# Gate and value products of the first MoE by Strassen's seven block products, with joins kept in PSUM and one ring of weight buffers

## The chip, the cores and the metric

The kernel runs on one core of a Trainium2 chip. The engines of the core are PE (TensorE: matmuls), DVE (VectorE), ACT (ScalarE), POOL (GpSimd) and SP (SyncE, which issues the loads and stores); each works through its own instructions in order. Matmul results are written to PSUM, in banks of 2 KB a partition; everything else lies in SBUF. The metric is the time of one execution on the device in microseconds, as a median over several runs.

## The reference

An attention over clusters (2 batches, 8 heads, 768 positions) gives 1536 tokens of 512 features. Two MoE layers follow, both in fp32:

```python
def _moe_ref(x, w_gate, w_val, w_out, rms_g):       # 512 -> 1536 -> 512
    rms = np.sqrt(np.mean(x * x, axis=-1, keepdims=True) + 1e-06)
    xn = x / rms * rms_g
    g = xn @ w_gate
    silu = g * (1.0 / (1.0 + np.exp(-g)))
    val = xn @ w_val
    return (silu * val @ w_out).astype(np.float32)

def _moe2_ref(x, w_in, w_out, s, b):                # 512 -> 2048 -> 512
    h = x @ w_in
    r = np.maximum(h, 0.0)
    g = s * (r * r) + b
    return (g @ w_out).astype(np.float32)
```

The weights come as 64-bit floats; the kernel turns them to 32 bits itself.

## The kernel before, in words

**Products.** An fp32 product is made of three fp32r matmuls: each operand is split in a high part (ACT copies it to fp32r) and a low part (operand less high part, on POOL or DVE), and high x high, high x low and low x high are summed in PSUM. The tokens form four blocks `t` of 384 (`TB`), the d_ff features tiles `f` of 128, and two neighbouring tiles are a pair `fs`. A gate and value unit (`unit1`, matmuls in `mm3`, L728) of one `f` and one `t` is 24 matmuls. A projection (`proj`, `project_mm`, L740 in the first MoE, L742 in the second) of one pair and one `t` is 24 matmuls in the first and 18 in the second; DVE adds each of its results to `acc` (L750).

**Weights.** A weight tile is loaded as raw 64-bit words (`load_w`, SP), ACT makes two ramps of its top bytes (L710, L711), DVE two bit operations (L713, L716) that give the 32-bit value, then ACT makes the high and POOL the low part (L719, L722). `add_pair` does this for a pair of w_in tiles of the second MoE, with the sums of weight blocks that Strassen's method needs (L1158 to L1181).

**Strassen in the second MoE.** `quad2` computes a pair `fs` for half the tokens (two blocks `t`, together `u`) by seven block products of 6 matmuls (L1395), 42 in place of 48. It holds five banks: the first product is copied to SBUF by ACT (L1418), DVE joins the others to it (L1413), and the results are finished from there: ReLU and square (L1424, L1427, L1430), scale and shift on ACT (L1434), and the split in `gh` and `gl` (L1241, L1244) for the projection. The sums of input blocks ("forms", `forms_` and `forms_last`) are made once for each `u`.

**Order.** Up to about 288 us a planner (`Plan`, `pl`) orders the attention together with the first two pairs of the first MoE for the first two blocks `t`. What follows is ordered by `Post`, which fills each engine's queue by earliest start and due time from written-in durations; PE's order is that in which the code adds the steps. An operation given to `either` goes to POOL, or to DVE where it would end sooner by more than `GAIN` (0). The loop over `items` at the end sets PE's order: for each pair of the first MoE and each `t` two units, then the projection of the `t` before; then for each pair of the second MoE and `u` a group of `quad2`, then the projections of the `u` before. Weight buffers are two sets, one for each second item (`s`).

## Time and profile before

| | |
|---|---|
| median of 3 runs | 806.29 us (803.33 to 806.7) |
| the profiled execution | 807.27 us, its span 805.5 us, granted clock 0.994 |
| attention with the first units | 0 to about 290 us |
| first MoE | about 290 to 541 us |
| second MoE | about 541 to 803 us |

A row of the chain of waits reads: start in us, length in us, engine, tile written, line, number of instructions run together. A group row reads: line, engine, operation, what is written and read, shape, count, busy time in us and mean ns of one, then idle time in front of it and what ended that. `po` and `pg` are PSUM banks, `hv`, `th` temporary tiles, `wa`, `wb` the weights in work. A row of the windows has the count of instructions in brackets behind each busy time; PEclk is the granted clock of TensorE as a share of full speed.

### The profile page before, as it was taken

Reading aid. Unit: us, or ns where it says so; the run is one execution under the profiler, and the core shown is the slowest. Engines: PE = TensorE matmul, PEld = TensorE weight load, DVE = VectorE, ACT = ScalarE, POOL = GpSimd, SP = SyncE. Lnnn points to the kernel's source line nnn. Section 1 sums busy time; section 2 is a strip of 40 time slices with the busy share of each in tenths; the row PEclk is TensorE's granted clock in tenths of the full one; section 3 lists DMA queues with packets and bytes.
Section 4 is the critical chain, followed back from the end, with each engine's and each line's share of the span. In section 5 each row is a group of like instructions: output and inputs, shape, how many; then the busy total and the mean of one; then the engine's idle time right before and its main releaser. Section 6 shows DMA issues by size and latency. Waiting matters only on the chain.

```text
span 805.5 us, 14231 instructions
## 1 busy us (share of the span) xinstructions
PE 765.4 (95%) x5409; PEld 704.2 (87%) x5409; DVE 616.2 (76%) x979; ACT 470.4 (58%) x901; POOL 461.3 (57%) x418
## 2 busy tenths in 40 slices
PE   3899999899999899999999999998999999999998
PEld 1688876789998889999999999997888888988986
DVE  6899887988776657777755646598888878889775
ACT  5478798657757635564533413456656666576541
...
GB/s 116 93 137 119 136 172 124 64 121 118 107 108 32 49 27 121 109 111 108 128 79 27 106 27 53 53 1 26 27 53 79 74 57 77 56 79 52 53 2 156
DMA packets 98820, 65.14 MB, mean 81 GB/s; under 512 B 64992, under 2 KB 89664, under 8 KB 98752
## 3 DMA queue, kind: packets, MB, share of 16 engines
...
## 4 chain that ended last, share of the span: by engine, by line
PE 77%; DVE 10%; POOL 7%; issue 3%; ACT 2%; DMA 1%; SPq 0%; DVEq 0%; POOLq 0%; ACTq 0%
PE pg L728 23%; PE po L742 16%; PE pg L1395 11%; PE po L740 9%; PE mps L515 4%; PE pv L586 3%; PE sps L546 3%; POOL al L563 3%; PE sps L547 2%; DVE mt L523 2%; PE pv L576 2%; PE pg L740 2%; DVE wa L713 1%; POOL ah L557 1%; DVE xn L640 1%
## 5 line engine op out<-in xcount | busy, mean ns | idle before, releaser
L1244 POOL TENSOR_TENSOR gl<-hv,gh 128x384 fp32r<-128x384 f32 x73 | 82.5, 1135 | 119.5 <-ACT gh L1241 119.5
L563 POOL TENSOR_TENSOR al<-a,ah 128x768 f16<-128x768 f32 x80 | 135.6, 1712 | 18.9 <-ACT ah L559 18.1
L722 POOL TENSOR_TENSOR wl<-wa,wh 128x512 fp32r<-128x512 f32 x58 | 75.7, 1308 | 104.3 <-ACT wh L719 94.2
L728 PE MATMUL pg<-xh,wh 128*128 128x384 f32 x384 | 130.1, 339 | 2.6 <-DVE xl L656 1.4
L728 PE MATMUL pg<-xh,wl 128*128 128x384 f32 x384 | 129.2, 337 | 0.0
L728 PE MATMUL pg<-xl,wh 128*128 128x384 f32 x384 | 129.0, 336 | 0.0
L750 DVE TENSOR_TENSOR acc<-po,acc 128x512 f32<-128x512 f32 (+1 forms) x156 | 97.1, 625 | 37.7 <-PE po L742 19.3
L552 ACT ACTIVATE a<-sps 128x384 f32<-128x384 f32 x192 | 86.2, 488 | 30.7 <-PE sps L547 28.4
L523 DVE TENSOR_REDUCE mt<-mps 128x1 fp32r<-128x768 f32 x96 | 90.2, 947 | 13.8 <-PE mps L515 12.7
L728 PEld LDWEIGHTS pg<-xh,wh 128*128 128x128 f32 x384 | 72.6, 189 | 3.5 <-DVE xl L656 1.7
L742 PE MATMUL po<-wh,gl 128*128 128x512 f32 x192 | 75.0, 391 | 0.0
L742 PE MATMUL po<-wl,gh 128*128 128x512 f32 x192 | 75.0, 390 | 0.0
L742 PE MATMUL po<-wh,gh 128*128 128x512 f32 x192 | 74.7, 389 | 0.0
L546 PE MATMUL sps<-q 128*128 128x384 f32 x192 | 70.7, 368 | 3.7 <-DVE ot L497 1.7
L728 PEld LDWEIGHTS pg<-xl,wh 128*128 128x128 f32 x384 | 72.6, 189 | 0.0
L1241 ACT ACTIVATE gh<-hv 128x384 fp32r<-128x384 f32 x104 | 52.7, 519 | 34.0 <-DVE hv L1232 33.0
L728 PEld LDWEIGHTS pg<-xh,wl 128*128 128x128 f32 x384 | 72.5, 189 | 0.0
L713 DVE SCALAR_TENSOR_TENSOR wa<-wb,wa 128x512 int32<-128x512 f32 x52 | 53.2, 1023 | 18.9 <-ACT wb L711 13.3
L547 PE MATMUL sps<-q 128*128 128x384 f32 x192 | 64.7, 337 | 0.0
L515 PE MATMUL mps<-q 127*128 127x384 f32 x192 | 56.8, 387 | 5.0 <-DVE mt L523 2.9
L719 ACT ACTIVATE wh<-wa 128x512 fp32r<-128x512 f32 x58 | 36.3, 628 | 35.6 <-DVE wa L716 29.1
L586 PEld LDWEIGHTS <-ah 128*128 128x128 f16 x960 | 47.3, 98 | 7.0 <-issue 5.9
...
## 6 DMA issues: line engine op xcount, KB each, us to landing
...
```

Of the source, the lines that this page charges most:

```text
L515: nc.tensor.matmul(ps[:, e, 0:HALF], lhsT=x[0:127, 1, c * 128:c * 128 + 128], rhs=x[0:127, 2, e * HALF:(e + 1) * HALF], start=True, stop=T ...
L523: nc.vector.tensor_reduce(out=mt_of[i][:, c:c + 1], in_=m_t.pop((i, c))[:, :, 0:HALF], axis=AX.XY, op=ALU.max)
L546: nc.tensor.matmul(ps[:, 0:HALF], lhsT=x[:, 2, ks], rhs=x[:, 1, cs], start=True, stop=False)
L547: nc.tensor.matmul(ps[:, 0:HALF], lhsT=x[:, 3, ks], rhs=x[:, 0, cs], start=False, stop=True)
L552: act(out=a_t[i, c][:, e * HALF:(e + 1) * HALF], in_=s_t.pop((i, c, e))[:, 0:HALF], func=ACTF.Exp, scale=scale)
L563: nc.gpsimd.tensor_tensor(out=al, in0=a_t.pop((i, c)), in1=ah_t[i, c], op=ALU.subtract)
L728: nc.tensor.matmul(ps, lhsT=a[:, kk * 128:kk * 128 + 128], rhs=x[:, kk, :], start=(kk == m == 0), stop=(kk == KC - 1 and m == 2),)
L740: nc.tensor.matmul(ps, lhsT=a[:, cs], rhs=x, start=st[0], stop=st[1])
L742: nc.tensor.matmul(ps, lhsT=x[:, cs], rhs=a, start=st[0], stop=st[1])
L750: tt(out=ac, in0=ps, in1=ac, op=ALU.add)
L1244: two(eng)(out=gl, in0=src(), in1=gh.bitcast(F32), op=ALU.subtract)
L1395: nc.tensor.matmul(B(x), lhsT=a[:, k_ * 128:k_ * 128 + 128], rhs=b[:, k_], start=(not more and k_ == m == 0), stop=(k_ == 1 and m == 2), s ...
```

## The change

Outside the attention, the gate and value products of the first MoE are computed by Strassen's method too, one group of 42 matmuls (`quad`) for the gate and one for the value of a pair and a half `u` of the tokens: 9 of these (pair, `u`), 18 groups. Pair 1 for `t` 2 and 3 stays plain. `quad` serves both MoEs; its last three joins write to the PSUM bank that they read, and `gate1`, `val1` or `finish2` takes the result from there. `forms1` makes the input forms from the high and low parts that exist; those for `u` 0, first half, are added to the attention's planner. Weights of gate and value go through `add_pair`; all split weights share a ring of 24 tiles (`slot`). `Post` starts from the times at which the first planner ends each engine, and `GAIN` is 0.75. `finish2` has ACT make the ReLU and DVE the square, from PSUM, for all results of the second MoE. The core of the diff:

```diff
-GAIN = 0.0
+GAIN = 0.75
...
+    def forms1(u, add, lone, ks=(0, 1)):
+
+
+        def alloc():
+            views(1, u, (xh[2 * u], xl[2 * u]), (xh[2 * u + 1], xl[2 * u + 1]), new_e(u))
+            C[1, u, "t1"] = C[1, u, "12"]
+
+        e = (f"e{u}", 1)
+        if 0 in ks:
+            add("AL", 0.0, alloc, lone[0], [e, *(lone[1])], [e])
+        for k_ in ks:
+            x = lambda name, k_=k_: [at(1, u, name, y, k_) for y in "hl"]
+            xk = lambda name, k_=k_: x_keys(u, 1, name, (k_,))
+            T = Temps(add, (1, u, k_), to=lambda name, k_=k_: [z[:, k_] for z in C[1, u, name]], keys=xk, e=e)
+            T.sum("tA", *x("12"), xk("12"), ALU.add, new=True)
+            T.sum("tB", *x("11"), xk("11"), ALU.add, new=True)
+            T.sum("tA", "tA", "tB")
+            T.sum("tC", *x("22"), xk("22"), ALU.add, new=True)
+            T.sum("tC", "tC", "tA")
+            T.split("tC", "t2")
+            T.sum("tB", "tC", "tB")
+            T.split("tB", "t3")
+            T.split("tA", "t1", ([xk("12")[0], *lone[2]], [xk("12")[1], *lone[3]]))
+            T.sum("tA", *x("21"), xk("21"), ALU.add, new=True)
+            T.sum("tA", "tC", "tA")
+            T.split("tA", "t4")
...
+        def split(self, name, form, more=((), ())):
+            src, key, (hk, lk) = self.of(self.key[name]), self.key[name], self.keys(form)
+
+            def hi():
+                act(out=self.to(form)[0], in_=src(), func=ACTF.Copy)
+
+            def lo(on):
+                h, l = self.to(form)
+                two(on)(out=l, in0=src(), in1=h.bitcast(F32), op=ALU.subtract)
+
+            self.add("ACT", .52, hi, [key, self.e], [hk, *more[0]])
+            self.add("POOL", 1.08, lo, [key, hk], [lk, *more[1]])
...
+    def last_pv():
+        att_b.close()
+        expp[0] = pool(ctx, "exp0", side="right")
+        spare.append(pool(ctx, "spare", side="right"))
...
+    def slot(n=[0]):
+
+
+        n[0] += 1
+        name = f"w{'hl'[(n[0] - 1) % 2]}{(n[0] - 1) % 6 // 2}"
+        return wp[(n[0] - 1) % 24 < 12].tile([128, 512], F32R, tag=name, name=name)
...
         def room(x):
-            temp[2, n, u, x] = tp[names[x]].tile([128, TB], F32, tag="hv", name="hv")
-
-        def join(to, x, y, op=ALU.add, turn=False):
+            temp[q, x] = tp[x == "u3"].tile([128, TB], F32, tag="hv", name="hv", bufs=2 - (x == "u3"))
+
+        def join(to, x, y, sign=1.0):
+            at, k_ = (lambda: V(to), vk[to]) if to in vk else (lambda: B(to), gk[to])
             def fn():
-                if to not in (y,):
+                if to != y and to in vk:
                     room(to)
-                a, b = (V(y), B(x)) if turn else (B(x), V(y))
-                tt(out=V(to), in0=a, in1=b, op=op)
-            then("DVE", .56, fn, [gk[x], vk[y]], [vk[to]], () if to == y else [vk[to]])
+                if sc == sign == 1.0:
+                    tt(out=at(), in0=B(x), in1=V(y), op=ALU.add)
+                else:
+                    stt(out=at(), in0=B(x), scalar=sc * sign, in1=V(y), op0=ALU.mult, op1=ALU.add)
+            then("DVE", .56, fn, [gk[x], vk[y]], [k_], [k_] if to in vk and to != y else ())
 
         def copy():
             room("u2")
-            act(out=V("u2"), in_=B("a"), func=ACTF.Copy)
...
+        def fin(x, p, t):
+            finish(fs[p], t, p, lambda: B(x), gk[x], 1.0 if x != "a" else sc)
 
         t0, t1 = 2 * u, 2 * u + 1
         prod("a", "11", "11")
...
         prod("c", "s3", "t3")
         join("u3", "c", "u2")
         prod("a", "12", "21", True)
-        finish(0, lambda: B("a"), gk["a"], "c11", 0, fs[0], t0)
+        fin("a", 0, t0)
         prod("d", "s1", "t1")
-        join("c22", "d", "u3")
-        finish(0, lambda: V("c22"), vk["c22"], "c22", 1, fs[1], t1)
+        join("c", "d", "u3")
+        fin("c", 1, t1)
         prod("e", "22", "t4")
-        join("u3", "e", "u3", ALU.subtract, True)
-        finish(0, lambda: V("u3"), vk["u3"], "u3", 1, fs[1], t0)
+        join("e", "e", "u3", -1.0)
+        fin("e", 1, t0)
         prod("d", "s4", "22", True)
-        join("u2", "d", "u2")
-        finish(0, lambda: V("u2"), vk["u2"], "u2", 0, fs[0], t1)
-
-    for (f, t), x in list(hs_t.items()):
-        hs_t[1, f, t] = x
-    items = [(1, pairs[1][NI], range(NX // 3, NTB)), *((1, fs, range(2, NTB)) for fs in pairs[1][:NI]),
-             *((1, fs, range(NTB)) for fs in pairs[1][NI + 1:-1]), (1, pairs[1][-1], (2, 3, 0, 1)), *((2, fs, (1, 0)) for fs in pairs[2])]
+        join("d", "d", "u2")
+        fin("d", 0, t1)
...
+    def gate1(f, t, p, src, sk, sc):
+        th = (f"th{p}", (1, f, t))
+        def tanh():
+            temp["th", f, t] = tp[p].tile([128, TB], F32, tag="th", name="th")
+            act(out=temp["th", f, t], in_=src(), func=ACTF.Tanh, scale=0.5)
+        def gate():
+            th_ = temp["th", f, t]
+            stt(out=th_, in0=th_, scalar=1.0, in1=src(), op0=ALU.add, op1=ALU.mult)
+        then("ACT", .48, tanh, [sk], [th], [th])
+        then("DVE", .56, gate, [sk], [th])
+
+    def val1(f, t, p, src, sk, sc):
+        th = (f"th{p}", (1, f, t))
+        def mul():
+            th_ = temp["th", f, t]
+            stt(out=th_, in0=th_, scalar=sc, in1=src(), op0=ALU.mult, op1=ALU.mult)
+        then("DVE", .56, mul, [sk], [th])
+        split_h(1, f, t, p, lambda: temp["th", f, t], th)
+
+    def finish2(f, t, p, src, sk, sc):
+        th = (f"th{p}", (2, f, t))
+        def relu():
+            temp["th2", f, t] = tp[p].tile([128, TB], F32, tag="th", name="th")
+            act(out=temp["th2", f, t], in_=src(), func=ACTF.Relu)
+        def square():
+            th_ = temp["th2", f, t]
+            stt(out=th_, in0=src(), scalar=0.0, in1=th_, op0=ALU.max, op1=ALU.mult)
+        def affine():
+            th_ = temp["th2", f, t]
+            act(out=th_, in_=th_, func=ACTF.Identity, scale=s_col, bias=b_col)
+        then("ACT", .48, relu, [sk], [th], [th])
+        then("DVE", .56, square, [sk], [th])
+        then("ACT", .7, affine, [], [th])
+        split_h(2, f, t, p, lambda: temp["th2", f, t], th)
+
+    late1, rest1 = pairs[1][:NI], pairs[1][NI + 1:]
+    items = [(1, rest1[0], (0, 1)), *((1, fs, (1,)) for fs in late1), *((1, fs, (0, 1)) for fs in rest1[1:-1]),
+             (1, last_pair, (1, 0)), *((2, fs, (1, 0)) for fs in pairs[2])]
...
+    for kind, fs, _ in items:
+        weights_of(kind, fs)
+    fs = pairs[1][NI]
+    later(1, fs, 1, (0, 0))
+    flush()
+    for t in (2, 3):
+        for p, f in enumerate(fs):
+            unit1(f, t, p)
+        later(1, fs, t)
+    forms1(0, add1, ((), (), (), ()), (1,))
+    forms1(1, add1, ([k_ for t in (2, 3) for k_ in plain(t)], (), (), ()))
+    for kind, fs, us in items:
+        for u in us:
             if kind == 1:
-                old = k_ == 0 and t < 2
-                ps = (0, 0) if old else (0, 1)
-                for p, f in enumerate(fs):
-                    if not old:
-                        unit1(f, t, s, p)
-                m = count[t]
-                count[t] += 2
-                pend.append(lambda a=(1, fs, t, s, 1, ps, m == 0, m + 2 == NF[1]): proj(*a))
-                if len(pend) > 1:
-                    pend.pop(0)()
+                quad(1, 0, fs, u, 1.0, gate1)
+                if fs is last_pair and u == us[0]:
+                    quad(1, 1, fs, u, 0.5, val1)
+                    for t in (2 * u, 2 * u + 1):
+                        later(1, fs, t)
+                    flush()
+                    continue
+                flush()
+                quad(1, 1, fs, u, 0.5, val1)
             else:
-                if fs[0] == 0 and t != blocks[0]:
-                    flush(1)
-                quad2(fs, t, s)
+                if fs[0] == 0 and u == us[1]:
+                    flush(0)
+                quad(2, 0, fs, u, 1.0, finish2)
                 flush()
-                for e in range(2):
-                    pend.append(lambda a=(2, fs, 2 * t + e, s, 2, (0, 1), fs[0] == 0, fs[0] + 2 == NF[2]): proj(*a))
-        if k_ + 1 < len(items):
-            kind, fs, _ = items[k_ + 1]
-            pieces = [(f, j) for j, f in ((0, fs[0]), (1, fs[0]), (0, fs[1]), (1, fs[1]), (2, fs[0]), (2, fs[1]))] if kind == 1 else [None, (fs[0], 1), (fs[1], 1)]
-            for i, x in enumerate(pieces):
-                prio = begin + (now[0] - begin) * i / len(pieces)
-                if x is None:
-                    add_pair(fs, 1 - s, prio)
-                else:
-                    add_w(kind, x[0], x[1], 1 - s, x[1] if kind == 1 else 2, prio)
+            for t in (2 * u, 2 * u + 1) if fs is last_pair else (2 * u + 1, 2 * u):
+                later(kind, fs, t)
     flush()
     sched = tc.manual_schedule()
     sched.__enter__()
```

Three places of the order that this gives (a number behind a name is its buffer). The first is PE at the end of the attention, where the last transposes `tr` of the input end; L740 and L746 are the projection, L728 a unit. Before:

```order
L740 MATMUL pg<-gl,wh 128x384
L740 MATMUL pg<-gh,wl 128x384
L647 MATMUL tr<-ident,xn 128x128 x8
L728 MATMUL pg<-xh,wh 128x384
L728 MATMUL pg<-xl,wh 128x384
L728 MATMUL pg<-xh,wl 128x384
```

and with the change:

```order
L746 MATMUL pg<-gl,wh 128x384
L746 MATMUL pg<-gh,wl 128x384
L655 MATMUL tr<-ident,xn 128x128 x8
L746 MATMUL po<-gh,wh 128x384
L746 MATMUL po<-gl,wh 128x384
L746 MATMUL po<-gh,wl 128x384
```

The projection of pair 1 for `t` 1 has moved from behind the first unit after the attention to ahead of it.

The second is POOL at the same place; L563 is attention work, L722 and L728 are lower parts of weights, L982 and L988 the lower parts `gl` of the last units of the attention's planner, L1128 and L1140 sums and lower parts of forms. Before:

```order
L563 TENSOR_TENSOR al_4533<-a_4457,ah_4481 128x768
L563 TENSOR_TENSOR al_4540<-a_4465,ah_4535 128x768
L722 TENSOR_TENSOR wl1_4582<-wa_4388,wh1_4538 128x512
L722 TENSOR_TENSOR wl2_4657<-wa_4612,wh2_4651 128x512
L982 TENSOR_TENSOR gl_4655<-hv_4474,gh_4654 128x384
L982 TENSOR_TENSOR gl_4714<-hv_4667,gh_4713 128x384
L982 TENSOR_TENSOR gl_4793<-hv_4734,gh_4792 128x384
```

and with the change:

```order
L1128 TENSOR_TENSOR tB_4658<-xh0_2540,xl0_2541 128x384
L728 TENSOR_TENSOR wl2_4672<-wa_4612,wh2_4666 128x512
L988 TENSOR_TENSOR gl_4670<-hv_4474,gh_4669 128x384
L1128 TENSOR_TENSOR tA_4655<-tA_4655,tB_4658 128x384
L1128 TENSOR_TENSOR tC_4714<-xh1_2542,xl1_2543 128x384
L1128 TENSOR_TENSOR tC_4714<-tC_4714,tA_4655 128x384
L988 TENSOR_TENSOR gl_4733<-hv_4682,gh_4732 128x384
L1140 TENSOR_TENSOR el0_4647<-tC_4714,eh0_4646 128x384
L1128 TENSOR_TENSOR tB_4658<-tC_4714,tB_4658 128x384
L1140 TENSOR_TENSOR el0_4647<-tB_4658,eh0_4646 128x384
L1140 TENSOR_TENSOR xl1_2543<-tA_4655,xh1_2542 128x384
L988 TENSOR_TENSOR gl_4819<-hv_4755,gh_4818 128x384
```

Up to the last `gl`, which the projection of pair 1 for `t` 1 reads, stand nine sums and splits of forms: eight in these rows and one `tA` just ahead of them.

The third is DVE in a value group of the first MoE; L713, L716 (now L1273, L1275) are bit operations on weights, L1232 the product of a unit, L1513 joins, L1557 the product with the gate. Before, in two units:

```order
L713 SCALAR_TENSOR_TENSOR wa_5682<-wb_5683,wa_5682 128x512
L1227 SCALAR_TENSOR_TENSOR th_5701<-th_5701,pg_5664 128x384
L716 SCALAR_TENSOR_TENSOR wa_5682<-raw_5628,wa_5682 128x512
L1232 SCALAR_TENSOR_TENSOR hv_5702<-th_5701,pg_5688 128x384
L713 SCALAR_TENSOR_TENSOR wa1_5721<-wb_5722,wa1_5721 128x512
```

and with the change:

```order
L1513 SCALAR_TENSOR_TENSOR hv_5622<-pg_5606,hv_5622 128x384
L1275 SCALAR_TENSOR_TENSOR wa_5600<-raw_5505,wa_5600 128x512
L1513 SCALAR_TENSOR_TENSOR hv_5642<-pg_5615,hv_5622 128x384
L1273 SCALAR_TENSOR_TENSOR wa1_5601<-wb_5602,wa1_5601 128x512
L1513 SCALAR_TENSOR_TENSOR pg_5615<-pg_5635,hv_5642 128x384
L1275 SCALAR_TENSOR_TENSOR wa1_5601<-raw_5547,wa1_5601 128x512
L1557 SCALAR_TENSOR_TENSOR th_5492<-th_5492,pg_5592 128x384
```

The bit operations now stand between the joins of a group; the third L1513 row is the join that frees the fourth bank, which the group's last product is written to.

## Rows read from the trace of the kernel before

**Rows 1.** The page, busy time, share and instructions by engine.
```profile
PE 765.4 (95%) x5409; PEld 704.2 (87%) x5409; DVE 616.2 (76%) x979; ACT 470.4 (58%) x901; POOL 461.3 (57%) x418
```

**Rows 2.** Chain of waits, first and second MoE: start us, us, engine, tile, line.
```profile
304.35 8.32 PE pg L728 x48
312.67 4.16 PE po L740 x24
...
572.83 7.30 PE pg L1395 x42
580.14 8.20 PE po L742 x36
```

**Rows 3.** Waits of PE after 290 us: waiting line, releaser: total us, times, longest.
```profile
PE pg L1395 <- DVE hv L1413: 3.5, 8, 0.8
PE pg L728 <- DVE xl L656: 1.4, 1, 1.4
PE pg L1395 <- DVE el L1286: 1.1, 1, 1.1
```

**Rows 4.** Windows: length, busy us of PE, PEld, DVE, ACT, POOL, PEclk, DMA, GB/s.
```profile
300.00:520.00 220.00, 220.00 (x1272) 220.00 (x1271) 145.59 (x227) 102.05 (x178) 79.13 (x68) 1.00 0.27 86
565.00:785.00 220.00, 217.28 (x1089) 195.52 (x1088) 182.13 (x277) 134.85 (x243) 111.44 (x106) 1.00 0.18 56
525.00:548.00 23.00, 22.71 (x131) 22.39 (x130) 20.60 (x30) 13.45 (x28) 20.98 (x17) 1.00 0.00 1
```

**Rows 5.** Chain of waits, the first unit after the attention.
```profile
290.03 10.15 PE pg L728 x48
```

**Rows 6.** Windows, the start of that unit.
```profile
290.00:292.00 2.00, 1.97 (x7) 1.97 (x8) 0.00 (x0) 0.00 (x0) 0.00 (x0) 0.62 0.00 0
```

**Rows 7.** Timeline of POOL: start us, us, instruction, idle before and its releaser.
```profile
278.53 1.02 POOL L982 TENSOR_TENSOR gl<-hv,gh 128x384 fp32r<-128x384 f32 x1 [3.73 <-ACT gh L978]
286.28 1.02 POOL L982 TENSOR_TENSOR gl<-hv,gh 128x384 fp32r<-128x384 f32 x1 [6.73 <-ACT gh L978]
297.32 1.57 POOL L1244 TENSOR_TENSOR gl<-hv,gh 128x384 fp32r<-128x384 f32 x1 [10.02 <-ACT gh L1241]
...
304.80 1.28 POOL L722 TENSOR_TENSOR wl<-wa,wh 128x512 fp32r<-128x512 f32 x1 [2.36 <-ACT wh L719]
```

**Rows 8.** Groups of POOL, 300 to 520 us: busy us, mean ns, idle before.
```profile
L722 POOL TENSOR_TENSOR wl<-wa,wh 128x512 fp32r<-128x512 f32 x32 | 42.0, 1317 | 56.3 <-ACT wh L719 46.1 <-PE po L740 8.1 <-issue 2.1
L1244 POOL TENSOR_TENSOR gl<-hv,gh 128x384 fp32r<-128x384 f32 x24 | 27.7, 1153 | 70.0 <-ACT gh L1241 70.0
...
L1167 POOL TENSOR_TENSOR wb<-wa 128x256 f32<-128x256 f32 x2 | 1.5, 736 | 3.5 <-DVE wa L1160 3.5
```

**Rows 9.** Groups of DVE, 300 to 520 us; the last row 565 to 785.
```profile
L750 DVE TENSOR_TENSOR acc<-po,acc 128x384 f32<-128x384 f32 x64 | 35.1, 553 | 17.1 <-PE po L740 16.8
L713 DVE SCALAR_TENSOR_TENSOR wa<-wb,wa 128x512 int32<-128x512 f32 x31 | 29.8, 963 | 11.0 <-ACT wb L711 5.8 <-POOL wl L722 5.2
L716 DVE SCALAR_TENSOR_TENSOR wa<-raw,wa 128x512 int32<-128x512 int32 x31 | 29.0, 935 | 0.4
...
L1430 DVE SCALAR_TENSOR_TENSOR th<-hv 128x384 f32<-128x384 f32 x28 | 23.6, 847 | 0.0
```

**Rows 10.** Timeline of DVE around 304 us.
```profile
303.37 0.68 DVE L716 SCALAR_TENSOR_TENSOR wa<-raw,wa 128x512 int32<-128x512 int32 x1
303.97 1.01 DVE L750 TENSOR_TENSOR acc<-po,acc 128x384 f32<-128x384 f32 x2
304.90 1.73 DVE L713 SCALAR_TENSOR_TENSOR wa<-wb,wa 128x512 int32<-128x512 f32 x1
```

**Rows 11.** Chain of waits, one Strassen group of the second MoE.
```profile
603.85 3.16 PE pg L1395 x18
...
607.56 1.68 DVE wa L713
...
610.48 1.31 PE pg L1395 x6
```

More of the change, by code (lines that the diff above doesn't have):

```diff
@@ L147, in __init__, with add @@
         super().__init__(bufs)
-        self.alt = {}
+        self.alt, self.taken, self.free, self.ready, self.soon = {}, {}, {}, {}, {}
+    def add(self, eng, dur, fn, r=(), w=(), **more):
+        self.soon[len(self.ops)] = max((self.ready.get(key, -1e3) for key in r), default=-1e3)
+        super().add(eng, dur, fn, r, w, **more)
     def due(self):
-        ops, taken, after, t = self.ops, {}, {}, 0.0
+        ops, after, t = self.ops, {}, 0.0
+        taken = {k: list(v) for k, v in self.taken.items()}
         late = [1e9] * len(ops)
@@ L1079, in two, with then, either @@
-    def two(eng):
-        return tt if eng == "DVE" else gps
-    W, C, bank, temp = {}, {}, {}, {}
-    for t in range(NTB):
-        held((f"x{t}", 1))
-    for t in range(2):
-        held((f"acc{t}", 1))
+        post.add("PE", dur, fn, r=r, w=w, new=new)
+    def then(eng, dur, fn, r, w, new=(), lat=None):
+        post.add(eng, dur, fn, r=r, w=w, new=new, lat=lat)
+    def either(dur, d2, fn, r, w, new=()):
+        post.alt[len(post.ops)] = ("DVE", d2)
+        post.add("POOL", dur, fn, r=r, w=w, new=new)
@@ new lines, in add1, with w_keys, new_bank @@
+    def add1(eng, dur, fn, r, w, new=()):
+        if eng == "POOL":
+            either(dur, .97, fn, r, w, new)
+        else:
+            then(eng, dur, fn, r, w, new)
+    W, bank, temp = {}, {}, {}
+    def slot(n=[0]):
+        n[0] += 1
+        name = f"w{'hl'[(n[0] - 1) % 2]}{(n[0] - 1) % 6 // 2}"
+        return wp[(n[0] - 1) % 24 < 12].tile([128, 512], F32R, tag=name, name=name)
+    def w_keys(kind, f, j):
+        return [("w", (kind, f, j, x)) for x in "hl"]
+    def new_bank(key, p=None):
+        bank[key] = (p or ps_g[-1]).tile([128, 512], F32, tag="g", name="po" if p else "pg")
@@ L1102, in attention_moe_moe2_kernel @@
-    chain = {"load": None, "act": None}
+    for (f, t), x in list(hs_t.items()):
+        hs_t[1, f, t] = x
+    chain, turn = {"load": None, "act": None}, (x for _ in range(99) for x in ("wa", "sa"))
     def linked(what, key):
@@ new lines, in ramps, with hi, lo @@
+        def ramps():
+            st["a"] = wtmp.tile([128, 512], F32, tag="wa", name="wa") if side == "wa" else sap.tile([128, 512], F32, tag="wa1", name="wa1")
+            st["b"] = wtmp.tile([128, 512], F32, tag="wb", name="wb")
+            ramp(st["raw"], st["a"], st["b"])
+        def hi():
+            W[kind, f, 2] = slot(), slot()
+            act(out=W[kind, f, 2][0], in_=st["a"], func=ACTF.Copy)
+        def lo(eng):
+            h, l = W[kind, f, 2]
+            two(eng)(out=l, in0=st["a"], in1=h.bitcast(F32), op=ALU.subtract)
@@ L1190, in add_pair @@
             a = (a0, a1)[e]
[L1191 to L1194 removed]
+            then("ACT", 1.53, call(ramps, e), [raws[e], *(linked("act", ("wd", n)) if e == 0 else ())], [b, a],
+                 [wa, sa, wb] if e == 0 else ())
@@ L1276, in proj, with part_ @@
                 then("SP", .5, store, [(*tile, c)], [("out", t, c)])
-            if last and kind == 1 and t == last_t and c >= 2:
+            if z and c >= 2:
                 forms_last(t, c - 2)
-        if last and kind == 1 and t != last_t:
+        if end and t != last_t:
             forms_(t)
-    def part_(src, sk, to, ks, eng="POOL", more=0.0):
+    def part_(src, sk, u, name, k_, eng="POOL"):
+        hk, lk = x_keys(u, 2, name, (k_,))
+        to = lambda: [z[:, k_] for z in C[2, u, name]]
         def hi():
@@ new lines, in forms_last, with third @@
+        T, y = temps2(u, k_), lambda c: chunk(t - 1, c)
+        T.sum("tC", po[0], None, [ok[0]], new=True, eng="ACT")
+        T.sum("tA", po[0], y(k_), [ok[0], (*ac0, k_)], new=True, eng="DVE")
+        T.sum("tB", po[1], "tA", [ok[1]], new=True, eng="DVE")
+        T.split("tB", "t2")
+        T.split("tA", "t1")
+        def third(c=T.key["tC"]):
+            tt(out=po[0](), in0=po[1](), in1=T.tile[c], op=ALU.subtract)
+        then("DVE", .56, third, [ok[1], T.key["tC"]], [ok[0], ("third", k_)])
@@ L1388, in prod, with quad @@
+        part_(po[0], ok[0], u, "t3", k_, eng="DVE")
+        T.sum("tC", "tB", y(m), [(*ac0, m), ("third", k_)], new=True)
+        T.split("tC", "t4")
+        part_(po[1], ok[1], u, "22", k_, eng="DVE")
+    def quad(kind, j, fs, u, sc, finish):
+        q, n = (kind, j, fs[0], u), (kind, j, fs[0])
+        gk = {x: ("g", (q, x)) for x in "abcde"}
+        B = lambda x: bank[q, x][:, 0:TB]
         def prod(x, wn, xn, more=False):
```

437 lines of the change are left out of this document (204 added, 233 removed).

## The prediction

> **What bounds the kernel now.** I began with the busy shares of the page [rows 1]: PE is busy 95% of the span, DVE 76%, ACT 58%, POOL 57%. That is one average over three stages, so next I read the chain of waits, piece by piece, for the stage that is changed [rows 2]. From 304 us on it is PE's own work and nothing else: 8.32 us for the 48 matmuls of two gate and value units, 4.16 for the 24 of a projection, in turn up to 541 us; and in the second MoE 7.30 for a Strassen group of 42 and 8.20 for 36 projection matmuls. The list of PE's waits [rows 3] agrees: after 290 us there are 3.5 us in eight pieces in the second MoE, behind a join on DVE, one wait of 1.4 and one of 1.1. The table by windows says what is free beside PE [rows 4]: from 300 to 520 us PE has 220.00 of 220 us, DVE 145.59, ACT 102.05, POOL 79.13. From 565 to 785 us, with Strassen groups, PE still has 217.28 while DVE stands at 182.13. Between 525 and 548 us, where forms of the input are made for the second MoE, DVE is at 20.60 of 23 (90%) and POOL at 20.98 (91%), and PE has 22.71: the fullest stretch the trace has. So the first MoE is bound by the number of matmuls, and a saving there counts in full until DVE or POOL has no room left.
>
> **The change, part by part**
>
> *Matmuls.* Nine pairs of a feature pair and half the tokens, gate and value each, go from 48 to 42 matmuls: 18 groups, 108 matmuls. A group of 42 takes 7.30 us where 48 take 8.32 [rows 2], 0.174 us a matmul in both. 18 x 1.02 = **-18.4**. PE is the bound there, so no other work takes this up.
>
> *End of the attention.* Before, PE waits 1.4 us there [rows 3], for the low part of the last input block, and then does 48 matmuls in 10.15 us [rows 5] instead of 8.32: the granted clock stands at 0.62 of full in the first 2 us [rows 6], mostly the 1.2 GHz level. Now the 24 matmuls of a waiting projection stand ahead of the unit. They need nothing that is late: their last operand, the `gl` that POOL ends at 286.28 + 1.02 = 287.30 [rows 7], is there before 288.6. POOL has nine form operations more ahead of it, about 9 x 1.15 = 10.4 us; its idle time before 287 was 3.73 + 6.73 = 10.5 in the two gaps shown, so this just fits. The wait goes: **-1.4** (ends 0 and -1.4). With 4.16 us of matmuls in the hole the drop of the clock should go too: 10.15 - 8.32 = **-1.8** (ends 0 and -1.8).
>
> *POOL after the attention.* This is the dearest addition. The x forms of both halves of the tokens, the lower parts of weights and sums of weight blocks are wanted early. Counted in the changed order, POOL has 47 operations from that `gl` to the operands of the projection behind the third group: 34 of 128x384, 6 of 128x512 and 7 of 128x256. At 1.153, 1.317 and 0.736 us [rows 8] that is 39.2 + 7.9 + 5.2 = 52.3 us, so 339.6 us without a pause from 287.3. PE has 72 projection, 96 plain and 126 group matmuls up to there, 294 x 0.1735 = 51.0 us, from 288.6 to 339.6. They are level, and POOL waits for ACT's higher parts in between; at the share of the fullest stretch, 91%, it needs 57.4 us: **+5.1**. Ends: 0 (POOL without a pause) and +15, with the 34 at 1.57, the longest such in [rows 7]: 53.4 + 13.1 = 66.5.
>
> *DVE.* Over the 18 groups with their projections (18 x 7.30 + 18 x 4.16 = 206.3 us of PE) DVE has 234 operations with a PSUM source, 59 bit operations on weights and 25 sums or splits from SBUF alone. At the means of 0.553, 0.95 (963 and 935) and 0.847 us [rows 9] that is 129.4 + 56.1 + 21.2 = 206.7, level with PE. But two accumulations in a row took 1.01 us, not 1.11 [rows 10], so each in a full queue adds nearer 0.47: 110 + 56 + 21 = 187, 91%, the share of the fullest stretch. On the average DVE holds. By place it does not quite. A Strassen group's last product goes into the bank of the fourth, so PE waits until DVE has joined the fourth. In the second MoE bit operations get between: PE stopped after 18 matmuls of a second half begun at 603.85, DVE then did two bit operations (the first took 1.68) before the join, and PE went on at 610.48 [rows 11]. 36 matmuls end at 603.85 + 36 x 0.174 = 610.11, so 0.37 us are lost. In the changed order 12 of the 18 groups have bit or SBUF operations between the two joins, of the last twelve 7. 7 x 0.37 = **+2.6**; for the first six POOL's term above stands, and the two are not added. Ends: 0, and +8, which is the last twelve at the 0.92 share by the undiscounted prices (134.2 / 0.92 - 137.5).
>
> *Second MoE.* The square of a group's results goes from SBUF sources (0.847 us [rows 9], and some on POOL) to a ReLU on ACT and one DVE operation with a PSUM source, 0.553. That is 32 x 0.29 = 9 us off DVE, off the path as long as PE waits for joins alone. Two weight operations ahead of the critical join stand in 6 of 16 groups now, in 8 before: 2 x 0.37 = **-0.7** (ends -3.5, the whole entry of [rows 3], and +2 for new places).
>
> *At nothing:* ACT's 86 operations more, since ACT was busy 102 of 220 us [rows 4]; joins whose result is written to PSUM (their source was there already; the row for the same form is 0.55); the weight ring, since 24 slots hold what two sets held; loads, whose number stays. The turn to the second MoE: POOL has 14 operations there, 14 x 1.15 = 16 us, beside 8.2 + 7.3 us of PE, both projections and a group [rows 2], and the tail of what stands before: 0 (ends -1.1, the wait of [rows 3], and +3).
>
> **Sum.** The profiled execution took 807.3 us (its span 805.5), the median is 806.3, 1.0 lower. 807.3 - 18.4 - 1.4 - 1.8 + 5.1 + 2.6 - 0.7 = 792.7, as a median **792**.
>
> **The rivals**
>
> *Nothing stalls.* DVE and POOL fit, and the second MoE's waits go too: 807.3 - 18.4 - 3.2 - 3.5 - 1.0 = 781. For it: the stretch of rows 4 with 90% on both and PE at 99%. Against: 12 groups with operations in front of the join, and POOL level with PE at the start without any pause. Up to 786. 0.13.
>
> *DVE and POOL full.* The start costs up to 15 in place of 5.1, the last twelve groups up to 8 in place of 2.6: 792 + 9.9 + 5.4 = 807 at worst, from 797 on. For it: both sums come out level with PE at mean prices. 0.19.
>
> *POOL's share locks DVE (slower).* A bit operation took 0.68 us at 303.37 with POOL idle, and 1.73 at 304.90 beside POOL's operation of 304.80 [rows 7, 10]; operations with a PSUM source stay at 0.55. POOL's share in the first MoE rises from 79/220 to some 60%. If each of the 59 bit operations took 1.73, DVE would need 110 + 21 + 102 = 233 us beside 206 of PE, +27: 781 + 3.5 + 27 = 812. It decides from 1.70 us a bit operation on; the mean of [rows 9] is 0.95 at a POOL share of 36%, and 0.68 + 0.27 x 60/36 = 1.13, so this is far: 0.04. The Trainium skill, "SBUF — State Buffer", in the section "Who interferes with whom", says that a VectorE instruction with two SBUF inputs and a GpSimd instruction that reads SBUF use one shared port pair and that the one which comes second is blocked for the whole of the other. By that rule a bit operation's worst is its own 0.68 and one whole POOL operation, and the trace agrees where it shows both side by side.
>
> *It does not do what it says.* If something else (loads, or ACT's ramps) paced the first MoE, time would stay near 806. Rows 3 and 4 speak against it: 0.04.
>
> **How the numbers follow.** My forecast has 0.60 (786 to 797). The range of 8 in 10 leaves out the tail below 782 and that above 803, so **782 to 803**. About 0.5% (4 us) is what a measurement of this kernel can tell from no change. Faster, below 802.3: the forecast, the first rival and most of the second, 0.87. Same: the upper end of the second and the last, 0.09. Slower: the lock, 0.04.
>
> **What would show it.** Right: groups of 42 at 7.30 us in the first MoE; no hole at 288 us and a clock of 1.00 after it; waits of PE behind POOL's lower parts only in the first four groups, some 5 us; short waits of 0.3 to 0.6 behind a join after that. Wrong: PE waiting at the start by over 10 us, bit operations at a mean over 1.2 us, DVE busy over 95% from 350 to 500 us, or a low clock in a hole that the waits open.

## The result and the profile after

The changed kernel takes 791.64 us (median of 4 runs, 790.9 to 792.64), the one before, on the same chip, 805.47 (803.33 to 806.7). The ratio is 0.9832, 95% interval 0.9806 to 0.9858. The forecast was 792, from 782 to 803. The profiled execution of the changed kernel took 791.71 us, its span 790.0, 15.5 below the span before. Busy time by engine, which answers to [rows 1]:

```profile
PE 746.5 (94%) x5301; PEld 685.2 (87%) x5301; DVE 659.4 (83%) x1080; ACT 503.7 (64%) x987; POOL 564.2 (71%) x515
```

PE lost 18.9 us of busy time. DVE gained 43, ACT 33 and POOL 103, and the span is shorter all the same. The chain of waits in the first MoE, which answers to [rows 2]:

```profile
424.41 14.56 PE pg L1493 x84
438.97 8.32 PE po L746 x48
```

Two groups, value of one half and gate of the next, are 84 matmuls in 14.56 us, so 7.28 each where 8.32 stood: the price of the sum. Then the waits of PE after 290 us, beside [rows 3]:

```profile
PE pg L1493 <- DVE pg L1511: 4.8, 9, 1.6
PE pg L1493 <- ACT hv L1518: 2.5, 1, 2.5
PE pg L1493 <- DVE pg L1513: 1.8, 1, 1.8
PE pg L1493 <- DVE el L1140: 1.3, 1, 1.3
```

The 4.8 us in nine pieces behind a join are three kinds: one of 1.56 at the start, two of 0.48 and 0.86 later in the first MoE (in its fifth and its seventeenth group), and six of about 0.3 in the second. The 2.5 and the 1.8 belong to the start too. The windows, as in [rows 4]:

```profile
288.00:290.00 2.00, 2.00 (x13) 2.00 (x13) 1.65 (x3) 1.12 (x2) 1.28 (x3) 1.00 0.00 0
290.00:340.00 50.00, 44.16 (x252) 43.20 (x251) 44.05 (x62) 24.62 (x48) 49.45 (x42) 1.00 0.17 56
340.00:520.00 180.00, 178.54 (x1023) 176.78 (x1022) 162.14 (x276) 101.69 (x189) 119.67 (x112) 1.00 0.25 82
550.00:785.00 235.00, 231.76 (x1156) 208.01 (x1156) 189.70 (x298) 152.11 (x288) 124.00 (x115) 1.00 0.21 68
```

From 288 to 290 us, where PE had stood for 1.4 us before, it is full, at a clock of 1.00. From 290 to 340 us PE is idle for 5.84 us, while POOL is busy 49.45 of 50. From 340 to 520 us PE has 178.54 of 180 with DVE at 162.14 (90%): DVE held, as far as the forecast had asked.

The three stops of the start in PE's timeline (start, length, instruction, idle time before it and what ended that):

```profile
314.54 0.45 PE L1493 MATMUL pg<-xh,wh 128*128 128x384 f32 x1 [2.46 <-ACT hv L1518]
...
319.50 0.44 PE L1493 MATMUL pg<-xh,wh 128*128 128x384 f32 x1 [1.56 <-DVE pg L1511]
...
337.22 0.45 PE L1493 MATMUL pg<-xh,wl 128*128 128x384 f32 x1 [1.82 <-DVE pg L1513]
```

2.46 + 1.56 + 1.82 = 5.84 us. The first one shows how an engine that is late stops another that has time. POOL and then ACT, at the first of them:

```profile
310.92 1.33 POOL L1128 TENSOR_TENSOR tA<-tA,tB 128x384 f32<-128x384 f32 x1
```

```profile
308.37 0.47 ACT L1352 ACTIVATE th<-pg 128x384 f32<-128x384 f32 x1
312.28 0.52 ACT L1136 ACTIVATE xh<-tA 128x384 fp32r<-128x384 f32 x1 [3.44 <-POOL tA L1128]
312.71 0.75 ACT L1266 ACTIVATE wa<-raw,ebias 128x512 f32<-128x512 int8 x1
313.36 0.75 ACT L1267 ACTIVATE wb<-raw,ebias 128x512 f32<-128x512 int8 x1
314.02 0.47 ACT L1518 ACTIVATE hv<-pg 128x384 f32<-128x384 f32 x1
```

ACT does its work in order. The high part of a form (312.28) stands in its queue ahead of the copy of the first product, and waits 3.44 us for POOL's `tA`, which ends at 312.25. Behind it come two ramps, and the copy that PE waits for (L1518) starts at 314.02. Its product was there some 4 us earlier: PE did 12 more matmuls (2.1 us) before it stopped at 314.54 - 2.46 = 312.08.

The other two stops come ahead of the 37th of a group's 42 matmuls, the first of its last product, which needs the bank that a join on DVE frees. DVE ahead of the second stop and of the third:

```profile
317.95 0.56 DVE L1511 TENSOR_TENSOR hv<-pg,hv 128x384 f32<-128x384 f32 x1 [0.91 <-POOL gl L1372]
...
335.15 1.54 DVE L1273 SCALAR_TENSOR_TENSOR wa<-wb,wa 128x512 int32<-128x512 f32 x1
336.61 0.55 DVE L1513 SCALAR_TENSOR_TENSOR pg<-pg,hv 128x384 f32<-128x384 f32 x1
```

Ahead of the second DVE waits 0.91 us for POOL's `gl`; ahead of the third a bit operation of 1.54 us stands in front of the join.

### The profile page after: what moved, and what is told of

The parts are those of the page before. It is cut to its first block, busy times and chain, and to the rows that moved or that the text cites. A ratio compares the mean times of both kernels' runs of the same rounds, so it can differ in the third digit from the quotient of the medians.

```text
span 790.0 us, 14339 instructions
## 1 busy us (share of the span) xinstructions
PE 746.5 (94%) x5301; PEld 685.2 (87%) x5301; DVE 659.4 (83%) x1080; ACT 503.7 (64%) x987; POOL 564.2 (71%) x515
## 4 chain that ended last, share of the span: by engine, by line
PE 71%; DVE 12%; POOL 10%; issue 4%; ACT 2%; DMA 0%; DVEq 0%; POOLq 0%; ACTq 0%
PE pg L1493 25%; PE po L748 16%; PE po L746 8%; PE mps L523 4%; PE pv L594 4%; PE sps L554 3%; PE pg L734 3%; PE sps L555 3%; PE pv L584 2%; DVE mt L531 2%; POOL al L571 2%; PE pg L746 2%; DVE wa L1273 2%; DVE wa L1275 1%; POOL tA L1128 1%
## 5 line engine op out<-in xcount | busy, mean ns | idle before, releaser
L1372 POOL TENSOR_TENSOR gl<-th,gh 128x384 fp32r<-128x384 f32 x88 | 97.9, 1126 | 65.2 <-ACT gh L1369 55.4
L1493 PE MATMUL pg<-xh,wh 128*128 128x384 f32 x272 | 89.3, 338 | 6.3 <-DVE pg L1511 3.8
L1493 PE MATMUL pg<-xh,wl 128*128 128x384 f32 x272 | 89.0, 337 | 2.9 <-DVE pg L1513 1.8
L1493 PE MATMUL pg<-eh,wl 128*128 128x384 f32 x204 | 68.3, 335 | 0.1
L1493 PE MATMUL pg<-eh,wh 128*128 128x384 f32 x204 | 68.2, 334 | 0.0
L1273 DVE SCALAR_TENSOR_TENSOR wa<-wb,wa 128x512 int32<-128x512 f32 x62 | 64.1, 1034 | 0.3 <-ACT wb L1267 0.3
L1369 ACT ACTIVATE gh<-th 128x384 fp32r<-128x384 f32 x100 | 49.8, 517 | 18.6 <-DVE th L1557 17.6
L1275 DVE SCALAR_TENSOR_TENSOR wa<-raw,wa 128x512 int32<-128x512 int32 x62 | 57.7, 931 | 0.3
L1255 POOL TENSOR_TENSOR wl<-wa,wh 128x512 fp32r<-128x512 f32 x18 | 23.9, 1332 | 44.6 <-ACT wh L1251 44.6
L746 PE MATMUL po<-gh,wh 128*128 128x384 f32 x160 | 53.5, 335 | 0.0
L746 PE MATMUL po<-gl,wh 128*128 128x384 f32 x160 | 53.5, 334 | 0.0
```

The costliest lines, as they stand in the source:

```text
L746: nc.tensor.matmul(ps, lhsT=a[:, cs], rhs=x, start=st[0], stop=st[1])
L1273: stt(out=ai, in0=b, scalar=2.0 ** 31, in1=a, op0=ALU.min, op1=ALU.subtract, reverse1=True)
L1372: two(eng)(out=gl, in0=src(), in1=gh.bitcast(F32), op=ALU.subtract)
L1493: nc.tensor.matmul(B(x), lhsT=a[:, k_ * 128:k_ * 128 + 128], rhs=b[:, k_], start=(not more and k_ == m == 0), stop=(k_ == 1 and m == 2), s ...
```

## The experiments

Times are medians, ratios against the kernel before on the same chip in the same session. The sessions ran on different chips, so two versions are best compared by their ratios; the changed kernel has 0.9832 (0.9806 to 0.9858).

**1. Fewer forms.** Is it POOL's work that makes the stops? This version leaves out the second half of the forms of `u` 0, so its result is not that of the reference.

```diff
-                            B(x), lhsT=a[:, k_ * 128:k_ * 128 + 128], rhs=b[:, k_], start=(not more and k_ == m == 0),
+                            B(x), lhsT=a[:, k_ * 128:k_ * 128 + 128], rhs=b[:, 0 if (kind, u) == (1, 0) else k_], start=(not more and k_ == m == 0),
...
-    forms1(0, add1, ((), (), (), ()), (1,))
```

> Leaves out the second half (k 1) of the input forms for u 0 in the first MoE: the groups of u 0 read the first half in its place. 12 sums and splits fewer on POOL or DVE and 4 copies fewer on ACT just after the attention, the same matmuls. Theory (POOL's queue after the attention makes the three stops of PE at 314, 319 and 335 us, 5.84 us in all): POOL is done 12 x 1.2 = 14 us earlier, the stops shrink below 1.5 us in all, time 791.6 - 4.5 = about 787. Rival (the stops come from DVE, with its bit operations between joins, and from the order of ACT's queue): they stay at 4 us or more, time 790 to 792.

787.72 us, ratio 0.9792 (0.9776 to 0.9808). In the first 345 us one stop of PE is left:

```profile
315.93 0.44 PE L1493 MATMUL pg<-xh,wh 128*128 128x384 f32 x1 [1.03 <-DVE pg L1511]
```

1.03 in place of 5.84. By the two ratios the time fell by 3.2 us against the changed kernel, with intervals that just touch; a little came back as 0.64 and 1.24 us behind joins at 355 and 364 us. The work on the forms makes the stops. The run alone does not say on which engine: in its order POOL has nine operations fewer (506 for 515), DVE three (1077 for 1080) and ACT four (983 for 987). That POOL is the one the others wait for is read from the rows above.

**2. The projection behind the unit again.**

```diff
     later(1, fs, 1, (0, 0))
-    flush()
     for t in (2, 3):
         for p, f in enumerate(fs):
             unit1(f, t, p)
+        if t == 2:
+            flush()
         later(1, fs, t)
```

> Puts the waiting projection (24 matmuls) behind the first plain unit again, as before the change. The hole at 288 us should come back (1.4 us) and with it the low clock for some 20 matmuls after it (1.8 us). If the terms add, the time is 791.6 + 3.2 = 795. Theory: they do not all add, since the 3.2 us that PE loses there are 3.2 us more for POOL, whose lateness makes the later stops of 5.84 us: these shrink to some 2.6 and the time stays within 1 us of 791.6. Rival: POOL is not what the stops wait for, and the time goes to 795.

791.54 us, ratio 0.9837 (0.9817 to 0.9858): no difference from the changed kernel. PE's timeline has the hole, and then smaller stops:

```profile
289.21 0.45 PE L734 MATMUL pg<-xh,wh 128*128 128x384 f32 x1 [1.41 <-DVE xl L664]
...
318.03 0.44 PE L1493 MATMUL pg<-xh,wh 128*128 128x384 f32 x1 [1.50 <-DVE pg L1511]
...
334.84 0.44 PE L1493 MATMUL pg<-xh,wl 128*128 128x384 f32 x1 [0.55 <-DVE pg L1513]
```

```profile
290.00:292.00 2.00, 2.00 (x14) 2.00 (x13) 1.35 (x3) 0.40 (x2) 1.33 (x2) 1.00 0.00 0
```

1.41 us at 289 are back. Up to 345 us the stops are 1.50, 0.55 and 0.42, together 2.47 in place of 5.84. What PE loses in the hole it does not lose later: the engines beside it go on meanwhile. The stops shrank by 3.37 us, more than the hole's 1.41, without a shorter time; this remainder is not resolved here. And the clock behind the hole stayed at 1.00: the second term that was expected to come back did not.

**3. The kernel before once more.** The low clock had not come back with the hole, so the kernel before was profiled a second time.

> The kernel before, profiled once more. The question is the 1.8 us that the low clock took behind the hole at 288 us. If the hole brings the low clock each time, the first unit behind it takes 10.1 us again. If it does not (the run with the hole put back showed none), the unit takes 8.3 us, and the 1.8 us belong to one execution and not to the change.

802.78 us in this execution (span 801.0), 4.5 us less than the profiled one of [rows 5]. The hole is the same 1.41 us. The chain behind it, and the window:

```profile
287.04 8.62 PE pg L728 x48
```

```profile
288.00:290.00 2.00, 2.00 (x14) 2.00 (x13) 0.03 (x1) 0.55 (x2) 0.00 (x0) 1.00 0.00 0
```

8.62 us for the unit in place of 10.15. The low clock of [rows 6] belongs to one execution. Another 3.0 us of the difference lie in the attention: its last transposes begin at 285.00 us here and at 287.99 in the first profile of the same kernel. In the changed kernel they begin at 287.43, and in its variants between 285.19 and 288.67, with one order of PE and DVE up to there. So single profiles are best compared from that point on.

**4. More for DVE.**

```diff
-GAIN = 0.75
+GAIN = 0.0
```

> GAIN 0 as before the change: the planner gives 32 operations more to DVE (1113 in place of 1081) and 32 fewer to POOL. Theory (POOL is the one that is late at the start, DVE has some 10% left): stops at the start shrink from 5.84 to some 3 us, but more DVE operations from SBUF stand in front of joins, each stop behind a join some 0.4 to 0.9 us, five to ten more of them: 789 to 794. Rival (DVE is what is full): stops behind joins grow to over 10 us in the first MoE, time over 797.

791.96 us, ratio 0.9865 (0.9814 to 0.9916; one of the four runs took 799.93). The stops change their place and do not shrink to the 3 us expected:

```profile
318.71 0.44 PE L1493 MATMUL pg<-xh,wh 128*128 128x384 f32 x1 [3.94 <-DVE pg L1511]
...
368.43 0.44 PE L1493 MATMUL pg<-xh,wh 128*128 128x384 f32 x1 [1.98 <-DVE pg L1511]
```

The first is one stop of 3.94 us instead of three, the second, at 368 us, has grown from 0.48. With POOL at 49.45 and DVE at 44.05 of 50 us in the changed kernel's start, moving work from one to the other gave nothing. With `GAIN` 0.3 the same came out:

> The changed kernel with GAIN 0.3 in place of 0.75, nothing else: 13 operations more on DVE. Between 0.75 (791.6) and 0 (792.0) no difference was measured, so 791 to 793; the stops at the start move from behind POOL to behind DVE.

792.6 us, ratio 0.9858 (0.9831 to 0.9884), with stops of 1.15, 3.82 and 1.97.

**5. The planner's own durations.**

```diff
-            self.add(eng or "POOL", {None: 1.08, "ACT": .48, "DVE": .56}[eng], fn, r, [key], [key] if new else ())
+            self.add(eng or "POOL", {None: 1.25, "ACT": .48, "DVE": .56}[eng], fn, r, [key], [key] if new else ())
...
-        then("DVE", .72, lambda: bits(0, st["raw"], st["a"], st["b"]), [b], [key])
-        then("DVE", .97, lambda: bits(1, st["raw"], st["a"], st["b"]), [raw], [key, ("wd", n)])
+        then("DVE", 1.0, lambda: bits(0, st["raw"], st["a"], st["b"]), [b], [key])
+        then("DVE", .93, lambda: bits(1, st["raw"], st["a"], st["b"]), [raw], [key, ("wd", n)])
...
```

`add_pair` has the same two numbers changed, and its sums of weight blocks go from 1.46 to 1.56.

> The planner's written-in durations set to what the trace shows in the first MoE (first bit operation 1.0 in place of 0.72, second 0.93 for 0.97, sums of forms 1.25 for 1.08, sums of weight blocks 1.56 for 1.46). Same work. Theory (the stops at the start are POOL's lack of time, not a bad order): little changes, 790 to 793. Rival (they come from an order made on wrong durations, such as ACT's copy of a first product behind a form that is late): the 2.5 us stop at 314 goes, time about 788.5.

794.9 us, ratio 0.9883 (0.9869 to 0.9898), by the two ratios 4.1 us slower than the changed kernel, with the 2.5 us stop gone as the rival said, but 1.49 and 1.07 us of new ones at 370 and 390 us and 2.44 at 561. The attention's planner takes the duration of a sum too: PE waits 1.42 us ahead of the last transposes, where the changed kernel has 0.29. Both expectations missed: the order made from truer mean durations was slower. Why is not settled here.

**6. DVE waits for the urgent operation.**

```diff
-        lag, look = {**LATENCY, "AL": 0.0}, dict(zip((*ENGINES, "AL"), (*P["look"], 0.0)))
+        lag, look = {**LATENCY, "AL": 0.0}, {**dict(zip((*ENGINES, "AL"), (*P["look"], 0.0))), "DVE": 0.9}
```

> In the second planner DVE may leave a ready operation aside for a more urgent one that starts within 0.9 us (0.11 before), so that fewer bit operations stand in front of joins; same work. Theory (short stops behind joins, 0.31 us each in the second MoE, come from two bit operations ahead of the join): they go from five of 0.3 to one or none, -1.5 us, but DVE idles a little more and the first MoE, where it is 90% busy, may give up to 3 us back: 789 to 794. Rival (order hardly matters, stops are where DVE has no time): stops stay as they are.

802.0 us, ratio 0.9966 (0.9951 to 0.998). The five stops of 0.31 us in the second MoE did go. The rest is worse than expected: 16 stops of 12.1 us in all between 320 and 540 us. A window of it, and the longest pause of DVE there:

```profile
315.00:340.00 25.00, 20.68 (x106) 19.41 (x105) 18.75 (x27) 11.95 (x24) 24.77 (x23) 0.93 0.18 60
```

```profile
323.91 1.60 DVE L1128 TENSOR_TENSOR tA<-tC,tA 128x384 f32<-128x384 f32 x1 [3.19 <-POOL tA L1128]
```

DVE is busy 18.75 of 25 us from 315 to 340, where the changed kernel has 23.46. It pauses 3.19 us for a sum on POOL, which has no pause itself (24.77 of 25), and 2.2 us in front of five copies of a projection's results. By the two ratios this order took back some 11 us of the 14 that the change had brought. The matmuls are the same; the planner gave POOL six operations that DVE had (521 and 1074, for 515 and 1080). Idle time of PE is only half of it: after 290 us PE waits 16.0 us in all, against 10.4 in the changed kernel. The other half is slower matmuls, with the clock at 0.93 in the window above and some 0.3 us behind every stop (see the next section).

**7. Sixteen groups.** Pair 0 stays plain for blocks 2 and 3, right behind pair 1's, with its gate and value weights made one by one:

```diff
...
-    items = [(1, rest1[0], (0, 1)), *((1, fs, (1,)) for fs in late1), *((1, fs, (0, 1)) for fs in rest1[1:-1]),
+    items = [*((1, fs, (0, 1)) for fs in rest1[:-1]),
...
+    for fs in late1:
+        for t in (2, 3):
+            for p, f in enumerate(fs):
+                unit1(f, t, p)
+            flush()
+            later(1, fs, t)
```

> Gate and value of pair 0 for the blocks 2 and 3 stay plain and come right behind the plain units of pair 1, so 16 groups instead of 18: 12 matmuls more, +2.0 us of PE. POOL has fewer sums and lower parts of weights at the start and some 25 us more of PE work beside it. Theory (POOL's lateness makes the stops at the start): they go from 5.84 us to under 1.5, time 791.6 + 2.0 - 4.6 = 789. Rival (the stops belong to the first groups wherever they stand, by DVE and the order of ACT's queue): they move some 25 us later and stay at 4 us or more, time about 793.

791.04 us, ratio 0.9828 (0.9801 to 0.9855), the same as the changed kernel. The stops up to 365 us:

```profile
321.86 0.44 PE L746 MATMUL po<-gh,wh 128*128 128x384 f32 x1 [2.05 <-DVE acc L754]
...
348.15 0.44 PE L1493 MATMUL pg<-xh,wh 128*128 128x384 f32 x1 [0.51 <-DVE pg L1511]
...
360.63 0.44 PE L1493 MATMUL pg<-xh,wl 128*128 128x384 f32 x1 [0.76 <-DVE pg L1513]
```

3.3 us, fewer than 5.84 and more than the 1.5 expected; 2.1 us of matmuls (12) were paid for 2.5. The first stop is new: eight copies of the projection's results stand on DVE behind the bit operations of the next weights. Spreading them failed:

```diff
-            flush()
+            flush(1)
             later(1, fs, t)
```

> Pair 0 plain for blocks 2 and 3, as in the run before, but the projections of 24 matmuls alternate with the plain units instead of standing 48 in a row, so that DVE's eight accumulations come in two lots. The 2.05 us stop of PE before a projection there, behind DVE's copies, should go: PE stops at the start some 1.3 us in place of 3.3, time 791.0 - 2.0 = 789. If DVE's bit operations stop PE elsewhere instead, the time stays at 791.

792.32 us, ratio 0.9846 (0.9827 to 0.9865), not shown to differ from the version before it. The stop there grew:

```profile
322.21 0.69 PE L746 MATMUL po<-gh,wh 128*128 128x384 f32 x1 [3.76 <-DVE acc L754]
```

With more given to DVE (`GAIN` 0.3):

> The same with GAIN 0.3: 15 operations more on DVE and 17 fewer on POOL. Theory (just after the attention both are nearly full, later DVE alone is near it): within 1 us of the run with GAIN 0.75; if POOL is the one that is late, 1 to 2 us faster.

790.17 us, ratio 0.9819 (0.9799 to 0.9838): the lowest of the versions that compute everything, but its interval overlaps that of the changed kernel (0.9806 to 0.9858), so it is not shown to be faster.

**8. The square from SBUF.**

```diff
-            stt(out=th_, in0=src(), scalar=0.0, in1=th_, op0=ALU.max, op1=ALU.mult)
+            stt(out=th_, in0=th_, scalar=0.0, in1=th_, op0=ALU.max, op1=ALU.mult)
```

> The square of the second MoE's results reads the ReLU from SBUF twice in place of PSUM once, as two of its four results did before the change: 64 DVE operations go from 0.55 to some 0.85 us, 19 us more of DVE in the second MoE. Theory (DVE there has room, and only the join ahead of the last product is waited for): stops of 1.6 us in that stage become 2 to 5 us, time 792 to 795. Rival (DVE is the bound): 797 or more.

790.88 us, ratio 0.9835 (0.9807 to 0.9863): no cost at all, below both expectations. The squares in the groups of DVE from 560 to 785 us, of the changed kernel and of this one, and POOL's commonest operation in both:

```profile
L1568 DVE SCALAR_TENSOR_TENSOR th<-pg,th 128x384 f32<-128x384 f32 x57 | 31.1, 548 | 3.4 <-ACT th L1565 3.4
```

```profile
L1568 DVE SCALAR_TENSOR_TENSOR th<-th 128x384 f32<-128x384 f32 x59 | 44.2, 752 | 3.2 <-ACT th L1565 2.9
```

```profile
L1372 POOL TENSOR_TENSOR gl<-th,gh 128x384 fp32r<-128x384 f32 x53 | 57.1, 1089 | 53.2 <-ACT gh L1369 43.4 <-PE pg L1493 9.0 <-POOL gl L1372 0.8
```

```profile
L1372 POOL TENSOR_TENSOR gl<-th,gh 128x384 fp32r<-128x384 f32 x53 | 63.9, 1217 | 48.3 <-ACT gh L1369 38.4 <-PE pg L1493 9.0 <-POOL gl L1372 0.7
```

The square went from 0.548 to 0.752 us, and POOL's lower parts beside it from 1.089 to 1.217. PE waits as before, five times 0.31 and once 0.17. DVE has that much room in the second MoE. One more thing is seen here, in the profiled execution, at 793.55 us the slowest of the four. Every engine has the order of the changed kernel, with the same instructions up to 530 us. The first stop is 2.42 us, and this time the clock falls behind it:

```profile
316.00:318.00 2.00, 2.00 (x11) 2.00 (x10) 2.00 (x3) 1.23 (x4) 2.00 (x3) 0.75 0.73 246
318.00:320.00 2.00, 2.00 (x8) 1.98 (x7) 1.10 (x4) 0.88 (x3) 2.00 (x2) 0.50 0.34 106
```

The second stop of 1.56 us is gone in return: PE was slow, and POOL caught up.

## Why the prediction was right, point by point

| term | forecast | measured, profile against profile |
|---|---|---|
| 108 matmuls fewer | -18.4 | -18.7 (108 x 14.56 / 84) |
| hole at the end of the attention | -1.4 | -1.4, but worth nothing by itself (experiment 2) |
| low clock behind it | -1.8 | -1.5 (10.15 - 8.62), of one execution, not of the change (3) |
| POOL after the attention, first six groups | +5.1 | +6.3 (5.84 + 0.48) |
| joins in the last twelve groups | +2.6 | +0.9 |
| joins in the second MoE | -0.7 | -1.6 |
| turn to the second MoE | 0 | +0.2 (1.3 for 1.1) |
| attention itself | 0 | -0.6, its own scatter |
| sum | -14.6 | -16.4; the spans differ by 15.5 |

The 0.9 us between the last two numbers are about what the sum of idle times leaves out: a stop costs some 0.3 us more than its idle time. From 314.54 to 317.94, where the second stop begins, PE does 18 matmuls in 3.40 us, where 18 x 0.1735 are 3.12, at a clock of 1.00; and the unit behind the hole took 8.62 in experiment 3, where 8.32 stand without a stop. The first MoE has five stops now where one hole was: 4 x 0.3 = 1.2 us by this estimate. The prediction had no term for it.

**The matmuls** came out as read from the chain, and nothing took them up. That was the step with the largest number and the surest ground: two rows of the same trace with 48 and 42 matmuls.

**POOL after the attention** was near in size (5.1 and 6.3), and the stretch was the right one: without 12 of the sums and splits the stops went to 1.03 us (experiment 1). That POOL needed the time forecast is in part luck. The first and the last of the 47 operations:

```profile
286.68 1.46 POOL L1128 TENSOR_TENSOR tA<-xh,xl 128x384 f32<-128x384 f32 x1
...
341.76 2.46 POOL L1372 TENSOR_TENSOR gl<-th,gh 128x384 fp32r<-128x384 f32 x2
```

From 286.68 to 344.22 are 57.5 us, where 57.4 were forecast. But the forecast had 52.3 / 47 = 1.11 us for one and POOL at 91%; the run has 57.5 / 47 = 1.22 and POOL at 99% (49.45 of 50 us). The two errors cancel. The way it acts was only half foreseen, too: none of the three stops is directly behind a lower part on POOL. The first is behind ACT and the second behind DVE, whose queues stand still for POOL. The third, 1.82 us, comes behind a join after bit operations of 1.50, 1.50 and 1.54 us beside POOL at 99%.

**The hole** is where the reasoning failed, though not the sum. "The wait goes: -1.4" treated a wait of PE ahead of POOL's long stretch as a term of its own. While POOL sets the pace, PE's arrival does not matter: with the hole put back the time stayed (791.54 and 791.64), and the stops behind it shrank by more than the hole's size. The +5.1 and the -1.4 were one term.

**The clock** is the second failed step: "With 4.16 us of matmuls in the hole the drop of the clock should go too". The row was real, but a second profile of the same kernel had the same hole and no drop. Seen from that execution (802.78 us) the change looks worth 11 us, from the median of the session 13.8; but 2.4 us of this are the end of the attention, at 285.00 there and at 287.43 in the changed kernel. From the last transposes on, with no low clock in either, it is 801.0 - 285.00 against 790.0 - 287.43, that is 13.4 us; the forecast's sum without the clock's term is 12.8. The forecast in absolute time held because the sum was made against an execution that had the drop, and took it off. That 792 met 791.64 so closely is luck: single terms were off by up to 1.7 us, to both sides.

**The joins.** 7 x 0.37 was too much for the last twelve groups; one stop came, 0.86. The rows of DVE show the difference between one operation and two in front of the join (428.04 in the first MoE; 623.86 and 625.57 in the second):

```profile
427.57 0.56 DVE L1513 SCALAR_TENSOR_TENSOR hv<-pg,hv 128x384 f32<-128x384 f32 x1 [0.41 <-PE pg L1493]
428.04 0.68 DVE L1273 SCALAR_TENSOR_TENSOR wa<-wb,wa 128x512 int32<-128x512 f32 x1
...
429.65 0.57 DVE L1513 SCALAR_TENSOR_TENSOR pg<-pg,hv 128x384 f32<-128x384 f32 x1 [0.46 <-PE pg L1493]
...
623.39 0.56 DVE L1511 TENSOR_TENSOR hv<-pg,hv 128x384 f32<-128x384 f32 x1 [0.41 <-PE pg L1493]
623.86 1.67 DVE L1273 SCALAR_TENSOR_TENSOR wa<-wb,wa 128x512 int32<-128x512 f32 x1
625.57 0.69 DVE L1275 SCALAR_TENSOR_TENSOR wa<-raw,wa 128x512 int32<-128x512 int32 x1
626.17 0.56 DVE L1511 TENSOR_TENSOR pg<-pg,hv 128x384 f32<-128x384 f32 x1
```

and POOL beside them:

```profile
430.01 1.01 POOL L1372 TENSOR_TENSOR gl<-th,gh 128x384 fp32r<-128x384 f32 x1 [4.01 <-ACT gh L1369]
...
623.69 1.29 POOL L1255 TENSOR_TENSOR wl<-wa,wh 128x512 fp32r<-128x512 f32 x1 [4.89 <-ACT wh L1251]
```

At 428.04 one bit operation stands between the two joins; it took 0.68, POOL was idle, and DVE then still waited 0.46 us for PE. At 623.86 there are two, and the first, beside POOL's operation of 623.69, took 1.67 us: the join came at 626.17, and PE had waited 0.32. One operation is enough where POOL is busy throughout, as ahead of the 0.48 us stop at 368 us (DVE, then POOL):

```profile
366.08 1.55 DVE L1273 SCALAR_TENSOR_TENSOR wa<-wb,wa 128x512 int32<-128x512 f32 x1
367.55 0.55 DVE L1511 TENSOR_TENSOR pg<-pg,hv 128x384 f32<-128x384 f32 x1
```

```profile
365.79 1.29 POOL L1316 TENSOR_TENSOR wh<-wa,wl 128x512 fp32r<-128x512 f32 x1
```

So in these rows the price hangs on whether the operations in front of the join meet POOL, and not on their number alone. The Trainium skill, "SBUF — State Buffer", section "Who interferes with whom", says that a VectorE operation with two SBUF inputs contends with a GpSimd operation that reads SBUF, and that the one which starts second is held up for the whole of the other. The trace agrees: POOL's operation, which started first, ends at 624.98, and the bit operation is over 0.55 us later, where 0.68 is its time undisturbed.

**The rivals.** DVE was not the bound (bit operations at a mean of 0.997 and 0.918 us from 300 to 520 us, where the slower case began at 1.70), POOL and DVE did not both fill up beyond the start, and stops did not vanish either.
